# Splitting expert weights one job per main step, with four result buffers

## The chip, the cores and the metric

The kernel runs on one core of one Trainium2 chip. The metric is device time in microseconds (us) of one execution; for the kernel before it is the median of 3 runs. The core's engines are named as the profile names them: PE (matmul) and PEld (its weight loads), DVE (VectorE), ACT (ScalarE), POOL (GpSimd) and SP (SyncE), which here issues nearly all DMA transfers.

## The reference, cut to what matters

Three layers follow each other. The first is a spectral filter along the sequence, the second a mixture of 8 experts with one expert per token, the third a dense MLP.

```python
X = np.fft.rfft(x, axis=1)                       # x: 8 x 3072 x 256
Yr = Xr @ w_r - Xi @ w_i + b_r
Yi = Xr @ w_i + Xi @ w_r + b_i
# soft threshold of both at 0.01, then irfft -> 24576 tokens of 256
expert_idx = np.argmax(xn @ en.T / tau, axis=1)
out[mask] = gate_w[mask, None] * (relu(x[mask] @ w1[e]) @ w2[e])   # w1: 8x256x1024, w2: 8x1024x256
g = leaky_relu(x @ w_in)                          # w_in: 256x2048
return g @ w_out
```

## The kernel before, in words

Products are made nearly exact in fp32 by splitting each operand into a rounded high part and a remainder (three matmuls for each product). The experts' weights are split once, by the kernel itself, in the shadow of the spectral layer: 128 jobs, 16 for each expert, each of one 128x256 block.

The spectral layer goes over 8 batches. A batch b has a **main stage** of 26 steps g (`main_step`, three of which, g = 0, 1, 2, are merged into the end of the stage before) and a **transform stage** of 37 steps n2. Every engine works its instructions off in the order in which they are written, SP's queue too: a transfer that has to wait holds all that is written behind it.

A main step g writes, in this order: `mix(g)`, six matmuls `pu` (L490), whose result ACT copies to `uh` (L178) and DVE subtracts to `ul` (L179); `s2(g-1)`, six matmuls `py` (L512) from `uh` and `ul`, then on DVE `z` (L515), `t` (L516) and `z` again (L517); from g = 24 on two `s1` of the next batch (matmuls `ps`, L468, which read that batch's input `xt`); `s2i(g-2)`, matmuls `pz` (L528) from `z`, with an ACT copy to `Z` (L531) in every second step; two small operations of the list `todo` (the gates of the batch before: a square root at L687 in step 3 and an exponential at L691 in step 5, both on ACT, and some DVE work); one `scatter`, or two where g is a multiple of 3 (POOL: a 1x1 copy `dummy` at L655 that waits for the step's `z`, then an indirect DMA `xs` at L656, which writes rows of the batch before to their slots in DRAM); then the **split jobs**; and in steps 21 to 24 of batches 1 to 6 `refill(b + 1, 0..3)`, which has SP load the first four pieces of the next batch's input (`load_x`, L369). Four more pieces are loaded in the transform stage. A batch's last two scatters are in its successor's transform stage.

A call of `split_job` has SP load a block `wf` (L451, 128 KB, three buffers). The call also works on the block that was loaded two calls earlier: ACT copies it to the high half of `hl` (L456), POOL subtracts for the low half (L457), and SP stores `hl` to DRAM (L458, 256 KB). So the load of a block waits for the subtraction of the block three jobs earlier, and the ACT copy into a buffer of `hl` for the store that last read this buffer: with two buffers, the store of two jobs earlier.

In batch 0 there is one call in each of the steps 4 to 25. From batch 1 on the calls are in steps 3 to 13: two in odd steps and one in even ones, 17 in a batch. Batch 0 does 22 jobs, batches 1 to 6 do 102, batch 7 the last 4. After the spectral layer come 103 expert blocks and 48 MLP tiles, which the change doesn't touch.

Of the kernel before, what the change touches and what calls it, by code (L numbers as in the profile page):

```python
# [12 lines left out]
F32R = mybir.dt.float32r  # L13
# [130 lines left out]
def build(ctx: ExitStack, tc: tile.TileContext, a: dict, out: bass.AP):  # L144
# [183 lines left out]
    def spectral(big, expert_start):  # L328
        with ExitStack() as st, ExitStack() as mst:
# [4 lines left out]
            m2 = mst.enter_context(tc.tile_pool(name="m2", bufs=2, side="right"))  # L334
# [62 lines left out]
            def prologue3():  # L397

                emb = rp.tile([E, D], F32, tag="lg", name="emb")
                trif = rp.tile([N1, 224], F32, tag="inc", name="trif")  # L400
                esq = rp.tile([E, D], F32, tag="ex", name="esq")
                en2 = rp.tile([E, 1], F32, tag="en2", name="en2")
                dma = lambda o, i: lambda: nc.sync.dma_start(o, i)

                def norm():
                    nc.scalar.activation(esq, emb, AF.Square, accum_out=en2)
                    nc.scalar.activation(en2, en2, AF.Sqrt)
                    nc.vector.tensor_scalar(en2, en2, 1e-6, None, op0=ALU.add)
                    nc.vector.reciprocal(en2, en2)
                    nc.vector.tensor_scalar(emb, emb, en2, None, op0=ALU.mult)  # L410

                def trans():

                    nc.vector.tensor_copy(identr, ident)
                    nc.vector.memset(en, 0.0)
                    pe_ = psb.tile([128, 2, E], F32, tag="b", name="pe_")
                    for db in range(2):
                        nc.tensor.transpose(pe_[:, db, :], emb[:, 128 * db:128 * db + 128], ident[:E, :E])
                    nc.vector.tensor_copy(en[:, :, 0:E], pe_)

                def init():
                    nc.vector.tensor_copy(tri, trif)
                    nc.vector.reciprocal(tau, tau)
                    nc.vector.memset(carry, 0.0)
                    nc.vector.memset(used, 0.0)

                return ([dma(emb, a["moe_expert_emb"]), dma(ident, a["ident"]),
                         dma(tau, a["moe_tau"][None, :].to_broadcast([128, 1])), norm,
                         dma(trif, a["tri"]), dma(scan, a["scan"]), dma(eord, a["eord"]), dma(li, a["li"]),
                         trans, init])  # L430
# [16 lines left out]
            def split_job():  # L447
                if jobs:
                    src, dst, o = jobs.pop()
                    wf = m3.tile([128, 256], F32, tag="wf", name="wf")  # L450
                    nc.sync.dma_start(wf, src)  # L451
                    wait.append((wf, dst, o))
                if len(wait) == 3 or not jobs and wait:
                    wf, dst, o = wait.pop(0)
                    hl = m2.tile([128, 2, 256], F32R, tag="hl", name="hl")
                    nc.scalar.activation(hl[:, 0], wf, AF.Copy)  # L456
                    nc.gpsimd.tensor_tensor(hl[:, 1], wf, hl[:, 0], op=ALU.subtract)  # L457
                    nc.sync.dma_start(dst.rearrange("p (s n) -> p s n", s=2)[:, :, o:o + 256], hl.bitcast(F32))  # L458
# [3 lines left out]
            def s1(b, n2, later=None):  # L462
                q, r = divmod(n2, 4)
                if n2 % 2 == 0:
                    ps1[0] = psa.tile([128, 2, 2, 96], F32, tag="a", name="ps1")
                p = ps1[0]
                for cb in range(2):
                    nc.tensor.matmul(p[:, n2 % 2, cb, :], xt[b, q][:, r, 128 * cb:128 * cb + 128],  # L468
                                     f1, start=True, stop=True)
                if n2 % 2 == 1:  # L470
                    src = p.rearrange("p n c j -> p c j n")
                    h = AH[:, :, :, n2 - 1:n2 + 1]
                    nc.scalar.activation(h, src, AF.Copy)
                    low = lambda: nc.vector.tensor_tensor(AL[:, :, :, n2 - 1:n2 + 1], src, h, op=ALU.subtract)
                    if later is None:
                        low()
                    else:
                        later.append(low)
# [3 lines left out]
            def mix(g):  # L482
                p = psa.tile([128, 512], F32, tag="a", name="pu")
                ops = []
                for cb in range(2):
                    ah = AH[:, cb, 4 * g:4 * g + 4, :].rearrange("p j n -> p (j n)")
                    al = AL[:, cb, 4 * g:4 * g + 4, :].rearrange("p j n -> p (j n)")
                    ops += [(ah, wh[:, cb]), (ah, wl[:, cb]), (al, wh[:, cb])]
                for i, (l, r) in enumerate(ops):
                    nc.tensor.matmul(p, l, r, start=(i == 0), stop=(i == 5))  # L490
                uh = m2.tile([128, 512], F32R, tag="uh", name="uh")
                ul = m2.tile([128, 512], F32R, tag="ul", name="ul")
                split_evict(uh, ul, p)
                U[g] = (uh, ul)
# [3 lines left out]
            def s2(g):  # L498
                uh, ul = U.pop(g)
                p = psb.tile([128, D], F32, tag="b", name="py2")  # L500
                if g == 0:
                    o1, o2 = 0, 128
                else:
                    o2 = 256 + (g - 1) * 192
                    o1 = o2 + 64
                ops = []
                for o, c in ((o1, 0), (o2, 256)):
                    ops += [(g2h[:, o:o + 128], uh[:, c:c + 256]),
                            (g2h[:, o:o + 128], ul[:, c:c + 256]),
                            (g2l[:, o:o + 128], uh[:, c:c + 256])]  # L510
                for i, (l, r) in enumerate(ops):
                    nc.tensor.matmul(p, l, r, start=(i == 0), stop=(i == 5))  # L512
                z = m2.tile([128, D], F32, tag="z", name="z", bufs=3)
                t = mp.tile([128, D], F32, tag="t", name="t")
                nc.vector.tensor_tensor(z, p, bt0 if g == 0 else bt, op=ALU.add)  # L515
                nc.vector.tensor_scalar(t, z, LAM, -LAM, op0=ALU.min, op1=ALU.max)  # L516
                nc.vector.tensor_tensor(z, z, t, op=ALU.subtract)  # L517
                Y[g] = z
# [3 lines left out]
            def s2i(g):  # L522
                y = Y.pop(g)
                if g % 2 == 0:
                    pz[0] = psc.tile([128, 2, 2, 128], F32, tag="c", name="pz")
                p = pz[0]
                for db in range(2):
                    nc.tensor.matmul(p[:, db, g % 2, :], y[:, 128 * db:128 * db + 128], gi[:, g, :],  # L528
                                     start=True, stop=True)
                if g % 2 == 1:  # L530
                    nc.scalar.activation(  # L531
                        Z[:, :, :, 4 * g - 4:4 * g + 4],
                        p.rearrange("p b g (j n) -> p b n (g j)", n=N2), AF.Copy)
# [294 lines left out]
            def main_step(b, g):  # L828
                last = b == B - 1
                if g == 3:  # L830

                    s2i(0)
                if g < NG:
                    mix(g)
                if 1 <= g <= NG:
                    s2(g - 1)
                if g >= NG and not last:
                    for _ in range(2):
                        s1(b + 1, lead[0])
                        lead[0] += 1  # L840
                if g >= 3:
                    s2i(g - 2)
                if b == 0 and g == 3:
                    todo.extend(prologue3())
                if g >= 3:
                    for _ in range(2):
                        if todo:
                            todo.pop(0)()
                if 2 <= g <= NG:
                    for _ in range(1 if g % 3 else 2):  # L850
                        scatter(Y[g - 1][0:1, 0:1])
                if g >= 4 if b == 0 else 3 <= g < 14:
                    split_job()
                    if b and g % 2:
                        split_job()
                if b == 0 and g % 3 == 1 and g // 3 < 8:
                    load_x(1, g // 3)
                if b and g in (21, 22, 23, 24):
                    refill(b + 1, g - 21)
# [340 lines left out]
```

## Time and profile before

| | |
|---|---|
| median of 3 runs | 4411.87 us (4411.73 to 4413.19) |
| profiled execution | 4420.32 us |
| its span in the trace | 4418.6 us |
| PE busy | 4293.5 us, 97% |
| DVE, ACT, POOL busy | 53%, 43%, 13% |
| spectral layer | about the first 1000 us of the span |

The table is read with the stages in mind: 97% for PE is a mean in which the long expert and MLP stages outweigh the spectral layer, where the change is.

### The profile page before, as it was taken

The numbers are of one execution on the slowest core, as the hardware profiler recorded it, in microseconds if no ns is written. First come the engines' busy times: TensorE is split into PE (matmuls) and PEld (weight loads), VectorE is DVE, ScalarE is ACT, GpSimd is POOL, SyncE is SP. The second block draws the span as 40 slices with busy tenths as digits, with TensorE's granted clock in tenths as the row PEclk, the third lists the DMA queues.
The fourth block names the chain that finished last, engine by engine and source line by source line (L and its number), as shares of the span: only waits on it lengthen the run. The fifth ranks groups of instructions, "written<-read, shape, count | busy, mean of one in ns | idle before, by whom it ended". The sixth has DMA issues, their size and how long they took to land.

```text
span 4418.6 us, 72633 instructions
## 1 busy us (share of the span) xinstructions
PE 4293.5 (97%) x27214; PEld 3813.2 (86%) x27214; DVE 2363.5 (53%) x4977; ACT 1891.4 (43%) x4268; POOL 595.1 (13%) x893
## 2 busy tenths in 40 slices
PE   9888889899999999999999999999999999999999
PEld 8777777779999999999978888888888888888888
DVE  5666666664455555543345555555555555555554
ACT  4455555443333333333344444444444444444443
POOL 2333333432100000000020001010100101010000
PEclk9999999999999999999999999999999999999999
DMA  7333333342332233433210000000000000000000
GB/s 217 100 113 94 93 99 99 117 144 95 107 109 86 94 137 131 170 120 117 85 40 20 29 20 25 24 25 24 23 27 20 26 23 25 24 24 25 20 20 15
DMA packets 139075, 309.72 MB, mean 70 GB/s; under 512 B 21049, under 2 KB 72866, under 8 KB 134370
## 3 DMA queue, kind: packets, MB, share of 16 engines
q1 hardware_dynamic: 113250, 244.34, 16.4%
q0 software_dynamic: 25472, 60.73, 4.6%
q8 instruction: 215, 3.52, 0.3%
q14 instruction: 138, 1.13, 0.1%
HBM read 542.30 MB, written 115.02 MB: 149 GB/s over the span
## 4 chain that ended last, share of the span: by engine, by line
PE 86%; DVE 4%; DMA 3%; issue 3%; ACT 2%; POOL 1%; another core or an unknown queue 0%; SPq 0%; ACTq 0%; POOLq 0%; DVEq 0%
PE mpH L1037 24%; PE mpO L1062 16%; PE pO L272 13%; PE pH L256 13%; PE mpO L1063 8%; PE pu L490 3%; PE py L512 1%; PE ps L468 1%; PE pz L528 1%; DMA w2d<-hl 1%; PE pyo L576 1%; DMA w1d<-hl 1%; DVE vl L543 1%; ACT uh L178 1%; PE pT L240 1%
## 5 line engine op out<-in xcount | busy, mean ns | idle before, releaser
L1062 PE MATMUL mpO<-W,mgh 128*128 128x512 f32 x3008 | 1096.5, 399 | 0.0
L1043 DVE TENSOR_TENSOR mg<-mpH,ms 128x512 f32<-128x512 f32 x768 | 531.2, 692 | 1047.8 <-ACT ms L1042 1043.1
L1037 PE MATMUL mpH<-mxh,W 128*128 128x512 f32 x3072 | 1083.5, 394 | 5.9 <-DVE mg L1043 4.7
L1042 ACT ACTIVATE ms<-mpH 128x512 f32<-128x512 f32 x768 | 459.9, 599 | 1191.0 <-PE mpH L1037 972.7
L1063 PE MATMUL mpO<-W,mgl 128*128 128x256 f32 x3008 | 842.3, 280 | 0.0
L256 PE MATMUL pH<-xh,W 128*128 128x256 f32 x3296 | 729.9, 284 | 3.2 <-issue 1.9
L1037 PEld LDWEIGHTS mpH<-mxh,W 128*128 128x128 f32 x3072 | 578.7, 188 | 146.0 <-DVE mg L1043 5.4
L1062 PEld LDWEIGHTS mpO<-W,mgh 128*128 128x128 f32 x3008 | 564.7, 188 | 132.5
L260 DVE SCALAR_TENSOR_TENSOR ehl<-pH,ehh 128x256 fp32r<-128x256 f32 x824 | 349.4, 424 | 606.4 <-ACT ehh L259 592.4
L259 ACT ACTIVATE ehh<-pH 128x256 fp32r<-128x256 f32 x824 | 316.4, 384 | 766.6 <-PE pH L256 754.6
L272 PE MATMUL pO<-W,ehh 128*128 128x256 f32 x3264 | 630.5, 285 | 0.0
L1037 PE MATMUL mpH<-mxl,W 128*128 128x512 f32 x1536 | 606.4, 395 | 0.0
L1063 PEld LDWEIGHTS mpO<-W,mgl 128*128 128x128 f32 x3008 | 567.3, 189 | 24.5
L256 PEld LDWEIGHTS pH<-xh,W 128*128 128x128 f32 x3296 | 574.2, 192 | 4.2 <-issue 1.8
L1010 POOL DMA_INDIRECT mxr<-ys,row x192 | 186.6, 972 | 2871.2 <-PE mpT L1022 1748.1
L1052 DVE TENSOR_TENSOR mgl<-mg,mgh 128x512 fp32r<-128x512 f32 x768 | 523.1, 681 | 0.0
L272 PEld LDWEIGHTS pO<-W,ehh 128*128 128x128 f32 x3264 | 508.7, 192 | 0.0
L1051 ACT ACTIVATE mgh<-mg 128x512 fp32r<-128x512 f32 x768 | 479.4, 624 | 0.1
L256 PE MATMUL pH<-xl,W 128*128 128x256 f32 x1648 | 467.1, 283 | 0.4 <-issue 0.4
L272 PE MATMUL pO<-W,ehl 128*128 128x256 f32 x1632 | 462.3, 283 | 0.0
L256 PEld LDWEIGHTS pH<-xl,W 128*128 128x128 f32 x1648 | 316.9, 192 | 1.2 <-issue 1.2
L1037 PEld LDWEIGHTS mpH<-mxl,W 128*128 128x128 f32 x1536 | 289.7, 189 | 32.7 <-issue 0.4
(214 smaller groups left out, 5370.2 us busy)
## 6 DMA issues: line engine op xcount, KB each, us to landing
W<-w1d SPq DMA_DIRECT2D x101, 2048.0 KB
W<-w2d SPq DMA_DIRECT2D x101, 2048.0 KB
xg<-xs SPq DMA_DIRECT2D x103, 256.0 KB
ys<-eo SPq DMA_DIRECT2D x102, 256.0 KB
xt<-in_x_dram SPq DMA_DIRECT2D x64, 384.0 KB
out_dram<-mo SPq DMA_DIRECT2D x47, 512.0 KB
wf<-in_moe_w_dram SPq DMA_DIRECT2D x128, 128.0 KB
w1d<-hl SPq DMA_DIRECT2D x64, 256.0 KB
```

What stands on the lines that cost most here:

```text
L256: nc.tensor.matmul(p, l, r, start=(i == 0), stop=(i == 5))
L259: nc.scalar.activation(hh, p, AF.Relu)
L260: nc.vector.scalar_tensor_tensor(hl, p, 0.0, hh, op0=ALU.max, op1=ALU.subtract)
L272: nc.tensor.matmul(O[b][:, t, :], l, r, start=(f == 0 and i == 0 and t == 0), stop=(f == 7 and i == 2 and t == 1))
L1010: nc.gpsimd.indirect_dma_start(out=xr[i][:, t].bitcast(F32), out_offset=None, in_=ys, in_offset=IndirectOffsetOnAxis(ap=slot[:, 4 * i + t: ...
L1037: nc.tensor.matmul(p, l, r, start=(j == 0), stop=(j == 5))
L1042: nc.scalar.activation(s, p, AF.Copy, scale=0.01)
L1043: nc.vector.tensor_tensor(g, p, s, op=ALU.max)
L1051: nc.scalar.activation(gh, g, AF.Copy)
L1052: nc.vector.tensor_tensor(gl, g, gh, op=ALU.subtract)
L1062: nc.tensor.matmul(p, gh[:, c], wout[:, :, f], start=(f == 0), stop=False)
L1063: nc.tensor.matmul(p[:, 0], gl[:, c], wout[:, 0, f], start=False, stop=(f == 15))
```

## The change

The single calls stay in steps 4 to 22 of batch 0 (23 to 25 go), and from batch 1 on there is one call in each of the steps 3 to 22, in place of 17 calls in steps 3 to 13. Batch 0 then does 19 jobs, batches 1 to 5 do 100, and batch 6 the last 9, with two more calls that only finish loaded blocks. `hl` gets four buffers, so that an ACT copy waits for the store of four jobs earlier.

```diff
-                    hl = m2.tile([128, 2, 256], F32R, tag="hl", name="hl")
+                    hl = m2.tile([128, 2, 256], F32R, tag="hl", name="hl", bufs=4)
...
-                if g >= 4 if b == 0 else 3 <= g < 14:
+                if 4 - (b > 0) <= g < 23:
                     split_job()
-                    if b and g % 2:
-                        split_job()
                 if b == 0 and g % 3 == 1 and g // 3 < 8:
                     load_x(1, g // 3)
                 if b and g in (21, 22, 23, 24):
                     refill(b + 1, g - 21)
```

## Rows read from the trace of the kernel before

**Rows 1.** The page, part 2: PE's busy tenths in 40 equal slices.
```profile
PE   9888889899999999999999999999999999999999
```
**Rows 2.** Windows from a batch's uh(3) to uh(23), L178 alone: stretch, length, busy.
```profile
core 0: us, ACT busy (x), PEclk, DMA share, GB/s
143.25:216.63 73.38, 11.66 (x20) 0.95 0.48 145
...
767.28:838.12 70.84, 11.63 (x21) 0.95 0.50 151
sum 429.60, ACT 69.80; mean ACT 11.63
...
55.97:89.16 33.19, 7.78 (x14) 1.00 0.67 202
894.50:952.38 57.88, 11.87 (x21) 1.00 0.35 114
```
**Rows 3.** Tile hl, whole span: durations, then what ended waits (us, times).
```profile
L456 ACT ACTIVATE hl<-wf x128: 399/417/424, 48.4 to 911.4; 128x256 fp32r<-128x256 f32 x128
...
  DMA w1d<-hl: 92.7, 37
  DMA w2d<-hl: 91.7, 38
```
**Rows 4.** Chain of waits, batch 2, main and transform stage: start, us, what.
```profile
283.21 2.38 DMA w2d<-hl
...
356.62 4.08 DMA xt<-in_x_dram
```
**Rows 5.** Timeline of ACT, steps 3 to 5 of batch 2 (idle before in brackets).
```profile
269.13 0.57 ACT L178 ACTIVATE uh<-pu 128x512 fp32r<-128x512 f32 x1
...
270.52 1.28 ACT L687 ACT_TABLE_LOAD   x1
...
271.95 0.71 ACT L456 ACTIVATE hl<-wf 128x256 fp32r<-128x256 f32 x2
272.56 0.57 ACT L178 ACTIVATE uh<-pu 128x512 fp32r<-128x512 f32 x1
277.92 0.42 ACT L456 ACTIVATE hl<-wf 128x256 fp32r<-128x256 f32 x1 [4.78 <-DMA w1d<-hl]
...
279.32 1.28 ACT L691 ACT_TABLE_LOAD   x1
```
**Rows 6.** Timeline of POOL, DVE and PE, steps 21 to 24 of batch 2.
```profile
336.76 0.17 POOL L655 COPY dummy<-z 1x1 f32<-1x1 f32 x1 [0.93 <-DVE z L517]
...
337.46 0.93 POOL L656 DMA_INDIRECT xs<-xt,si  x1 [0.53 <-issue]
...
338.73 0.92 POOL L656 DMA_INDIRECT xs<-xt,si  x1 [0.16 <-issue]
...
340.98 0.29 DVE L516 TENSOR_SCALAR t<-z 128x256 f32<-128x256 f32 x1
...
341.37 1.03 PE L468 MATMUL ps<-f,xt 96*128 96x96 f32 x8
```
**Rows 7.** Timelines of PE, POOL and DVE, steps 4 to 8 of batch 2.
```profile
276.74 1.10 PE L528 MATMUL pz<-gi,z 128*128 128x128 f32 x4 [1.96 <-DVE z L517]
...
287.57 0.74 POOL L457 TENSOR_TENSOR hl<-wf,hl 128x256 fp32r<-128x256 f32 x1
...
287.71 0.76 DVE L516 TENSOR_SCALAR t<-z 128x256 f32<-128x256 f32 x1
...
289.06 0.17 POOL L655 COPY dummy<-z 1x1 f32<-1x1 f32 x1 [0.75 <-DVE z L517]
```
**Rows 8.** Timeline of SP's queue, end of batch 2's split jobs.
```profile
317.06 0.54 SPq L458 DMA_DIRECT2D w1d<-hl  x1
317.65 0.60 SPq L451 DMA_DIRECT2D wf<-in_moe_w_dram  x1
...
322.58 1.80 SPq L369 DMA_DIRECT2D xt<-in_x_dram  x4
```

## The prediction, made before the change was run

> **What bounds the kernel now.** I read the page first. PE is busy nine tenths or more in most slices, but only eight tenths in slices 2 to 6 and in slice 8 [rows 1]; a slice is 110 us, so the holes lie in the spectral layer, where the change is. PE ends nearly everything else, and what the split jobs do can only be paid for, or won, in those holes.
>
> Next I took the pace of the main stage from the starts of `uh`, one in each step. In batch 0, with one job in each step and no scatters, 13 steps take 33.19 us, 2.55 each [rows 2]. That is the free pace: PE's own work. From batch 1 on the 20 steps from uh(3) to uh(23) would take 51.0 us at it. Batches 1 to 6 take 429.60 us together (the first and the last of six stretches stand in the rows), 123.6 more than 6 x 51.0. Batch 7, with only four jobs and the two finishing calls, takes 57.88, an excess of 6.9. So **130.5 us** of stalls lie in the steps that hold split jobs or follow them.
>
> The waits of tile `hl` name the cause: before its ACT copy, ACT sat idle for 92.7 + 91.7 us until a store of `hl` had landed, in 75 of 128 copies [rows 3]. The chain of waits shows one link: a store, 2.38 us from issue to landing, that releases the copy [rows 4]. With two buffers and three jobs in two steps, a copy waits for a store that POOL's subtraction made possible only just before. Behind the copy on ACT stands the next `uh`, behind that `ul`, `py` and PE.
>
> **What goes.** With four buffers a copy waits for the store of four jobs earlier, four steps or 10.2 us at the free pace. From `uh` to the end of a subtraction it takes, at two scatters, 6.2 us (below), and the store 2.4 more: 8.6, under 10.2. The whole wait of [rows 3] goes, in batches 1 to 7. I don't book its 184 us, since much of it overlaps work, but the 130.5 us of lost pace, and then subtract what stays or comes new.
>
> **What stays: the gates.** In step 3 ACT loads a table for the square root, 1.28 us, and makes two hl copies in 0.71; uh(4) comes 3.43 after uh(3), 0.9 late. In step 5 the exponential brings another table load of 1.28 [rows 5]. Neither goes with the change; only one copy of the two does. `z` is late behind `ul` too: PE waited 1.96 us for it in step 5 [rows 7]. Bounds for a batch: 0.9, the lateness of the one step, and 6.9, batch 7's whole excess with six jobs over two buffers. From 6.9 the wait for a store goes, 4.78 in the like place [rows 5], which leaves 2.1; I take 3.2 for what POOL still does to `z` there. Seven batches: 22.4.
>
> **What is new: POOL and SP in every step.** In three steps (7.65 us) POOL has four scatters and three subtractions. A scatter right behind another takes 1.27 (337.46 to 338.73), one after a wait 0.17 + 0.53 + 0.93 = 1.63 [rows 6]; a subtraction takes 0.74 [rows 7]. Run back to back that is 4 x 1.27 + 3 x 0.74 = 7.3, which just fits. With a wait ahead of each step's first scatter it is 8.4, and every step 0.25 longer: 17 steps, 4.2 a batch. POOL that lags runs back to back, so it should settle near the first. A `wf` load stands behind the store (0.59 apart on SP [rows 8]) and so behind a subtraction: 6.2 + 0.6 after `uh`, and with the 2.4 of the larger `hl` store as an upper bound it lands at 9.2. ACT needs it three steps on, and can start that copy as late as 2.1 behind its `uh` (2.55 less 0.42 for the copy [rows 3]), 9.75, so it fits by 0.5.
>
> There is a coupling to DVE: `t` takes 0.29 when free [rows 6], and 0.76 when it starts with a subtraction of 0.74 running; it ends 0.16 behind it [rows 7]. At the free pace `t` begins 1.7 after `uh`. The subtractions then lie 0.4, 2.4 or 1.9 into a step, so that only the third, in the step after next, comes near it, from behind. The Trainium skill (SBUF — State Buffer, "Who interferes with whom") says that a GpSimd instruction and a tensor_scalar in a two-port mode take the shared port pair whole, and that whoever comes second waits until the first is done. The trace agrees (0.76 against 0.29). By that rule a step in which the subtraction comes first loses up to 0.74 on DVE; where all do, it is the last rival below.
>
> For all of this I take 1.5 a batch, between 0 (batch 0 hides a job in every step) and 5 (4.2 plus a collision here and there). Five batches: 7.5. Batch 6 has jobs only to step 13; its share lies within the 3.2.
>
> **What is moved: the first input loads.** In steps 21 and 22 a call now stands ahead of the `refill` on SP, and its store waits for that step's subtraction. Before, SP had nothing left behind step 13's calls; four loads were issued at 322.58 [rows 8], 18.8 us ahead of the first `s1` at 341.37 [rows 6]. After, in batch 2's times with steps 21 to 23 already free: the second scatter of step 21 ends at 338.73 + 0.92 = 339.65, the subtraction 0.74 later at 340.4, 6.2 after uh(21) at 334.19 (uh(23) less two steps). The store goes out, and the first load 0.59 behind it, at 341.0. A first load of 384 KB took 4.08 from issue to landing [rows 4], which gives 345.1. PE wants it at 341.37 and is 3.7 us late; behind it wait all `ps` and the whole transform stage, which has nothing to catch up with. After idle time PE also starts slowly: the granted clock is 0.95 in the stretches with stalls against 1.00 without [rows 2]; I add an estimate of 0.5. So 4.2 in batches 1 to 5; batch 6 has done its jobs by then. Bounds 1.5 (the load lands in 2.4, as the smaller store does, and half of the rest is absorbed) and 5.5 (POOL lags by a further scatter). Five batches: 21. The later load of step 22 lands behind a stage that is shifted as far, and costs nothing more.
>
> **Nothing:** three calls fewer in batch 0, where PE waited little; two small `todo` operations in each of batch 6's steps, which DVE has room for; the four buffers themselves; the expert and MLP stages, which get the same data and start later or earlier as a whole.
>
> **The sum.** 130.5 - 22.4 - 7.5 - 21 = 79.6. The profiled execution took 4420.3 us, its span 4418.6; less 79.6 that is 4340.7. The median lies 8.4 below the profiled execution, so the forecast is 4411.9 - 79.6 = **4332** us, 1.8% faster.
>
> **The rivals.**
> - *The input load is hidden.* If SP or the load is quicker than I work out, or the transform stage has slack, the 21 us stay won: 4311. For it: the four loads were issued in a burst when they took 4.08, and a lone one may be quicker. Against: SP's order, and the need at 341.37.
> - *POOL becomes the bound.* If every step's first scatter pays the 0.53 of restart, or `wf` lands late, steps take 2.8 or a little more: 17 steps of 0.25 to 0.4 over five batches, 21 to 34 instead of 7.5: 4346 to 4359. For it: 7.3 of 7.65. Against: the restart cost vanishes when POOL lags.
> - *The loop through the shared port* (the other side). If each subtraction blocks the next step's `t`, the loop is: subtraction ends, rest of `t` and `z` 0.75 until `dummy` starts [rows 7], `dummy` to the end of the scatter 1.63, subtraction 0.74: 3.12, and 4.39 with two scatters. Twenty steps, seven of them double, take 71.3 instead of 51.0. Batches 1 to 5 then lose 20.3 + 4.2 each, where they lose 20.8 on average now (the 123.6 less batch 6's 19.8, over five): 18.5 us worse. Batch 6 with 11 such steps (39.4 against 28.1, a loss of 11.3) gains 8.5, batch 7 3.7. The gates' 3.2 comes on top in batches 1 to 6, 19: in all 4437. It decides at about three in four of the steps: the 130.5 less 21 (loads) and 22.4 (gates) over 111 steps is 0.78 a step, and a locked step costs 1.02. For it: `t` at 0.76 beside a subtraction. Against: once PE is slower, `t` is ready while POOL still scatters, and slips in ahead.
>
> **How the numbers follow.** Chances: forecast 0.48 (its own range 4318 to 4345), hidden load 0.27, POOL as the bound 0.20, the loop 0.05. The likeliest gives 4332. The range goes from the hidden load with gates and lag at the kind end (4311 less 9) to POOL as the bound with some collisions (4362), 4302 to 4362, leaving some 2 in 10 out on both sides. A change under 0.2% (9 us) could not be told from none; only the loop reaches there, whole or in part, so faster 0.95, same 0.02, slower 0.03.
>
> **What the changed profile would show.** Copies of `hl` no longer released by stores. `uh` every 2.55 us from about step 7 to step 23, and 54 to 57 us from uh(3) to uh(23) in batches 1 to 6. In batches 1 to 5, and not in 6, PE idle for 3 to 4 us ahead of the first `ps`, released by `xt`. `t` mostly at 0.29. The forecast is wrong if steps 8 to 22 run at 2.8 or more, if `t` is often near 1 us, if copies wait for `wf`, or if the wait ahead of `ps` is absent or above 5 us.

## The result, and the profile after

The changed kernel takes 4367.36 us (median of 4 runs, 4364.93 to 4374.58) against 4412.53 us for the kernel before, measured again on the same chip: ratio 0.9898, 95% interval 0.9881 to 0.9916. It is 45 us faster, where 80 were forecast (4332, range 4302 to 4362), and lies outside the range by 5 us. The main stages came out within 4 us of the forecast; the stretch behind them cost two and a half times what I had put down for it.

The same slices of the page as [rows 1], for the changed kernel: the holes in the spectral layer are fewer, not gone.

```profile
PE   9989898999999999999999999999999999999999
```

The windows of [rows 2] in the changed kernel, L178 alone, from uh(3) to uh(23) of batches 1 to 6 (first, last and sum), then of batch 7. Columns: stretch, its length, busy time (count), granted clock, DMA share, GB/s.

```profile
141.82:196.48 54.66, 11.80 (x21) 1.00 0.56 173
...
745.10:799.48 54.38, 11.86 (x20) 1.00 0.49 148
sum 338.82, ACT 70.84; mean ACT 11.81
...
851.84:903.03 51.19, 11.91 (x20) 1.00 0.28 90
```

The sum fell from 429.60 to 338.82, batch 7 from 57.88 to 51.19: 97.5 us are won here. 33.0 us of excess over the free pace are left (338.82 - 306, and 0.2 in batch 7); the forecast had 29.9.

Tile `hl` after, what ended its waits (us, times), against [rows 3]: no store is in the list any more. In its place stand the loads of `wf`.

```profile
  DMA wf<-in_moe_w_dram: 63.8, 56
  ACT hl L456: 31.3, 15
  issue: 6.8, 6
```

What was won is half given back behind uh(23). These are windows of PE from uh(23) of a batch to uh(3) of the next, first the kernel before, batches 1 to 6 (first, last, sum):

```profile
216.63:269.13 52.50, 49.13 (x402) 1.00 0.17 47
...
838.12:894.50 56.38, 53.39 (x402) 0.91 0.17 44
sum 321.65, PE 300.56; mean PE 50.09
```

and then the changed kernel, all six:

```profile
196.48:262.62 66.14, 57.23 (x402) 0.85 0.26 74
318.64:384.16 65.52, 57.75 (x402) 0.84 0.26 74
441.04:500.91 59.87, 51.89 (x402) 0.94 0.29 81
561.10:626.29 65.19, 57.94 (x402) 0.84 0.27 74
682.98:745.10 62.12, 53.15 (x402) 0.92 0.27 78
799.48:851.84 52.36, 49.16 (x402) 1.00 0.17 45
sum 371.20, PE 327.12; mean PE 54.52
```

Batches 1 to 5 lose 53.6 us together (318.8 against 265.3); batch 6, which has no split job after step 13, loses nothing, and even lacks the low clock that the kernel before shows there (4.0). The place is seen in the timelines of batch 2, of POOL, SP and PE in turn, which answer to [rows 6] and [rows 8]:

```profile
319.62 0.74 POOL L457 TENSOR_TENSOR hl<-wf,hl 128x256 fp32r<-128x256 f32 x1
...
320.38 0.54 SPq L458 DMA_DIRECT2D w1d<-hl  x1
321.22 0.35 SPq L369 DMA_DIRECT2D xt<-in_x_dram  x1
...
325.80 2.02 PE L468 MATMUL ps<-f,xt 96*128 96x96 f32 x8 [4.92 <-DMA xt<-in_x_dram]
```

The order is the one forecast: subtraction, store, first input load, and PE waiting for it. The wait is 4.94, 4.92, 4.47, 3.97 and 5.39 us in batches 1 to 5, 23.7 together. What was forecast far too small is seen in the row's duration: eight matmuls take 2.02 us, where the same eight took 1.03 in [rows 6]. Windows of PE in batch 2 (the fourth number is the granted clock) show why:

```profile
320.60:325.80 5.20, 0.28 (x3) 0.76 0.77 227
325.80:340.00 14.20, 14.20 (x69) 0.50 0.33 103
340.00:351.30 11.30, 10.22 (x93) 0.99 0.32 89
```

Behind the wait PE runs at 0.50 of its clock, 1.2 GHz, for 14 us, busy throughout. Over the five stretches PE idles 22.8 us more than before and is busy 30.9 us more, with the same work. The books of the profiled executions: 130.5 of stalls before, less 33.0 left, less 53.6 behind uh(23), plus 4.0 in batch 6, is 47.9; the spans differ by 51.9, the other 4 being small shifts ahead of batch 1 and after the spectral layer. The medians differ by 45.2.

### The profile page after: what moved, and what is told of

It reads as the page before. It is cut to its first block, busy times and chain, and to the rows that moved or that the text cites. A ratio compares the mean times of both kernels' runs of the same rounds, so it can differ in the third digit from the quotient of the medians.

```text
span 4366.7 us, 72634 instructions
## 1 busy us (share of the span) xinstructions
PE 4271.0 (98%) x27214; PEld 3819.4 (87%) x27214; DVE 2391.4 (55%) x4977; ACT 1895.8 (43%) x4268; POOL 601.2 (14%) x893
## 4 chain that ended last, share of the span: by engine, by line
PE 88%; DVE 5%; DMA 2%; issue 2%; ACT 1%; POOL 1%; SPq 0%; another core or an unknown queue 0%; DVEq 0%; POOLq 0%; ACTq 0%
PE mpH L1035 24%; PE mpO L1060 16%; PE pO L272 14%; PE pH L256 14%; PE mpO L1061 8%; PE pu L490 3%; PE ps L468 2%; PE py L512 1%; PE pz L528 1%; DMA xt<-in_x_dram 1%; PE pyo L576 1%; DVE t L516 1%; DVE z L517 1%; DVE vl L543 1%; PE pT L240 1%
```

## The experiments

Theory A: the first input load is late because it stands on SP behind the split stores of steps 21 and 22, and PE's idling brings the low clock on top. Rivals: the transfers themselves are slow there (B); the clock falls for another reason than the wait (C). For the main stages, theory W says that the waits for `wf` make up what is left there, and rival P that POOL does. The ratios are to the kernel before on the same chip, which took 4399.5 to 4411.4 us in these series. "Main" is the sum from uh(3) to uh(23) over batches 1 to 6 (306 at the free pace), "behind" the sum from uh(23) to the next uh(3); both are of one execution each, the profiled one.

| kernel | ratio (95% interval) | main, us | behind, us |
|---|---|---|---|
| before | 1 | 429.6 | 321.6 |
| changed | 0.9898 (0.9881 to 0.9916) | 338.8 | 371.2 |
| e1 loads early | 0.9822 (0.9804 to 0.9841) | 351.8 | 329.4 |
| e2 pace only | 0.9961 (0.9947 to 0.9976) | 365.2 | 360.7 |
| e3 buffers only | 0.9894 (0.9878 to 0.9911) | 384.1 | 320.2 |
| e4 kept warm | 0.9864 (0.9847 to 0.9880) | 338.4 | 357.7 |
| e5 one step ahead | 0.9799 (0.9783 to 0.9816) | 334.8 | 331.2 |
| e6 calls to 18 | 0.9786 (0.9770 to 0.9803) | 337.3 | 318.7 |
| e7 four blocks | 0.9873 (0.9856 to 0.9890) | 335.6 | 367.2 |
| e8 both | 0.9766 (0.9749 to 0.9782) | 329.6 | 319.1 |
| e9 idle long | 0.9908 (0.9892 to 0.9925) | 335.7 | 368.5 |
| e10 idle short | 0.9864 (0.9847 to 0.9881) | 335.8 | 354.8 |

**Loads early.** From the changed kernel:

```diff
+                if b and g in (17, 18, 19, 20):
+                    refill(b + 1, g - 17)
                 if 4 - (b > 0) <= g < 23:
                     split_job()
...
-                if b and g in (21, 22, 23, 24):
-                    refill(b + 1, g - 21)
```

> The changed kernel with the four refill loads of a batch written in steps 17 to 20, ahead of each step's split job, in place of steps 21 to 24 behind it. Theory A (the order on SP delays the first input load, PE idles ahead of the first ps for 4.0 to 5.4 us in batches 1 to 5, and then runs at a granted clock of 0.50 for some 14 us): the wait ahead of ps goes, the stretch from uh(23) to the next uh(3) falls from 60 to 66 us to the 52.5 of batch 6, and about 54 us go: 4313 (4305 to 4325). Rival B (the loads are late because subtractions, wf loads and stores now run up to the end of the stage and the transfers themselves are slow): a wait of 3 us or more stays and the time is above 4345. Rival C (the clock falls because the whole stage has less idle and more load, not through the wait): the wait goes, the granted clock of the transform stage stays below 0.9, and the time is about 4343.

The wait ahead of the first `ps` is gone and "behind" falls by 42 us, against rival B. But the input loads now stand among the `wf` loads on SP, and the main stages grow by 13 us. ACT's timeline in steps 18 to 21 of batch 2:

```profile
299.98 0.42 ACT L456 ACTIVATE hl<-wf 128x256 fp32r<-128x256 f32 x1 [2.38 <-DMA wf<-in_moe_w_dram]
...
307.92 0.42 ACT L456 ACTIVATE hl<-wf 128x256 fp32r<-128x256 f32 x1 [2.38 <-DMA wf<-in_moe_w_dram]
```

So the gain over the changed kernel is 0.8% where 1.2% was expected, and the time, 4336 us, lies above the expected range. In three of the later stages the clock falls here too, as it does now and then in the kernel before.

**The two edits apart.** "Pace only" gives `hl` two buffers again; "buffers only" is the kernel before with four.

```diff
-                    hl = m2.tile([128, 2, 256], F32R, tag="hl", name="hl", bufs=4)
+                    hl = m2.tile([128, 2, 256], F32R, tag="hl", name="hl")
```

> The changed kernel with two buffers for hl again: one call in each step, nothing else. If the wait for the store is what sets the pace (from uh to the end of a subtraction 6.2 us, the store 2.4 more, over two steps), steps run at about 4 us instead of 2.8, 20 steps lose about 29 us a batch where before 17 calls in 11 steps lost 20.8, and the late input load stays: 4440 (4410 to 4480), slower than before. If the spreading alone gives the gain and the buffers are spare, 4367 as the changed kernel.

```diff
-                    hl = m2.tile([128, 2, 256], F32R, tag="hl", name="hl")
+                    hl = m2.tile([128, 2, 256], F32R, tag="hl", name="hl", bufs=4)
```

> The kernel before with four buffers for hl and its old calls, 17 in steps 3 to 13. If the waits for the stores were all of the cost, the main stages get as short as in the changed kernel (54 to 57 us from uh(3) to uh(23)) and no input load is late: 4315. If POOL and the three wf buffers take the place of the store when three jobs come in two steps, steps 3 to 13 run at 3.5 to 4 us, copies wait for wf loads, and the time is about 4385 (4360 to 4405). In both cases no wait ahead of the first ps.

With the pace alone, copies still wait for stores, as tile `hl` shows, but the main stages lose 59 us where 174 (29 a batch) had been expected: steps follow each other at about 4.5, 2.0 and 2.7 us, three in 9.2, not at 4 each. The time is 4394 us where 4440 was expected, 0.4% faster than the kernel before and not slower. I had let every copy wait for the store of the slowest step.

```profile
  DMA w1d<-hl: 70.5, 43
  DMA w2d<-hl: 67.0, 41
```

With the buffers alone there is no wait ahead of `ps` and no wait for a store; ACT now waits for `wf` and for POOL:

```profile
  DMA wf<-in_moe_w_dram: 69.1, 53
  ACT hl L456: 36.6, 22
  POOL hl L457: 16.6, 15
```

The main stages win 45.5 us, nearly the whole gain: the kernel is as fast as both edits together, whose larger gain in the main stages is paid back behind them. The measured time lies below the 4385 of the expectation and within its bounds.

**Kept warm.** To part the clock from the wait, PE gets something to do while it waits:

```diff
+                if g == NG and 1 <= b <= 5:
+                    pk = psc.tile([128, 512], F32, tag="c", name="pk")
+                    for _ in range(18):
+                        nc.tensor.matmul(pk, wh[:, 0, :128], wh[:, 0], start=True, stop=True)
                 if g >= NG and not last:
```

> The changed kernel with 18 extra matmuls of 512 columns in step 24 of batches 1 to 5, ahead of the first s1; their result is not used. They fill some 4.1 us of the 4.0 to 5.4 us in which PE waits for the input. Theory A (the low clock behind the wait is the price of PE's idling): the wait in sum stays (PE busy in its place), but the granted clock behind it stays at 1.00, ps takes 0.58 instead of 1.01, and about 24 us go: 4343 (4335 to 4352). If the clock falls for another reason, or the idle time is the whole loss, no gain: 4367 or, where the extra matmuls are late themselves, up to 4375.

Windows of PE, 14.2 us from the first `ps` of batches 1 to 5:

```profile
204.47:218.67 14.20, 13.93 (x125) 1.00 0.35 104
317.75:331.95 14.20, 13.52 (x124) 1.00 0.42 117
435.73:449.93 14.20, 13.93 (x131) 1.00 0.27 80
553.49:567.69 14.20, 14.20 (x100) 0.76 0.34 105
675.32:689.52 14.20, 14.01 (x125) 1.00 0.39 112
```

The input is as late as before, yet the clock stays at 1.00 in four of five batches (in the changed kernel such windows show 0.51, 0.50, 0.82, 0.58 and 0.71). 13.5 us of "behind" go, where about 24 were expected, and the time, 4352 us, lies at the edge of the expected range. In batch 4 a wait of 1.4 us is left ahead of the first `ps`, and the clock falls behind it; in batches 4 and 5 it falls later in the stage, behind waits of 1.8 and 3.3 us for the second set of input loads.

**Idling alone.** Two kernels on top of "calls to 18" (below), where no input is late: POOL makes six (in the short one `range(3)`, three) extra subtractions on a scratch block, and PE reads the last one ahead of `ps`; nothing else uses it.

```diff
+                if g == NG and 1 <= b <= 5:
+                    pk = psc.tile([128, 512], F32, tag="c", name="pk")
+                    nc.tensor.matmul(pk, hold[0][:, :128], wh[:, 0], start=True, stop=True)
...
+                if g == NG - 1 and 1 <= b <= 5:
+                    hold[0] = mp.tile([128, 256], F32R, tag="hold", name="hold")
+                    for _ in range(6):
+                        nc.gpsimd.tensor_tensor(hold[0], wh[:, 0, :256], wl[:, 0, :256], op=ALU.subtract)
```

> The kernel with calls to step 18 (no late input load), in which PE is made to wait for nothing useful: in step 23 of batches 1 to 5 POOL makes six extra subtractions on a scratch block, ahead of its scatter, and in step 24 one extra matmul, not used, reads their result ahead of the first ps. The input is long there. If PE's idling itself costs the clock, PE idles about 4 us ahead of ps and then runs at a granted clock of 0.50 for some 14 us: the stretch from uh(23) to the next uh(3) goes from 52.5 to about 61 us in five batches, 45 us over the kernel with calls to step 18, about as slow as the changed kernel (ratio to the kernel before 0.989). If the clock falls only where DMA traffic or subtractions run beside PE at that time, only the idle time shows: 20 us over it, ratio 0.983.

> The same with three extra subtractions, so that PE idles about 1.8 us. If the price of the clock comes with any wait, 9 us of idling and about 25 of the clock in five batches, ratio 0.986. If it comes only with longer waits, as the waits of 1 to 2 us for the later input load let one think, the clock falls in one or two of the five batches and the ratio is 0.981 to 0.983.

The long one, PE's timeline in batch 2, the matmul that waits:

```profile
322.21 0.80 PE L839 MATMUL pk<-wh,hold 128*128 128x512 f32 x1 [4.36 <-POOL hold L855]
```

and the window of PE behind it:

```profile
322.21:336.41 14.20, 14.20 (x72) 0.54 0.07 21
```

With hardly any DMA traffic beside it (share 0.07), the clock falls in all five batches. They lose 49.7 us behind uh(23) against "calls to 18", 22.6 of it waiting (4.77 + 4.36 + 4.35 + 4.77 + 4.35) and 27.1 besides, 5.4 a batch: some 3 us of that are the extra matmuls themselves, the rest is the same work at the low clock. This is the changed kernel's loss, made by hand with no late input and hardly any DMA traffic, and together with "kept warm" it rules out rival C. The short one waits 1.9 us in each batch; of the windows behind, three show a clock near 0.52 and two 1.00, of which one each:

```profile
320.12:334.32 14.20, 14.20 (x70) 0.52 0.07 21
437.04:451.24 14.20, 13.93 (x125) 1.00 0.10 29
```

It costs almost what the reading "with any wait" had forecast (0.986), though the clock does not fall every time: in the two batches that kept it, a later wait for input of 3.1 and 1.4 us is followed by a dip of the clock.

**One step ahead.** Only the order of two statements in the changed kernel is exchanged:

```diff
+                if b and g in (21, 22, 23, 24):
+                    refill(b + 1, g - 21)
                 if 4 - (b > 0) <= g < 23:
                     split_job()
...
-                if b and g in (21, 22, 23, 24):
-                    refill(b + 1, g - 21)
```

> The changed kernel with refill written ahead of split_job in the same steps 21 to 24, so that the first input load stands behind the store of step 20's call and no longer behind that of step 21's. Theory A (the place on SP sets the delay, step by step): the load goes out about one step, 2.6 us, earlier; the wait ahead of the first ps falls from 4.0 to 5.4 to about 2.1 us in batches 1 to 5, 13 us in all, and what the clock takes behind it (now about 25 us) stays or goes with it: 4340 (4328 to 4355). Rival B (the transfers are slow in that stretch wherever the load stands): the wait stays above 3.5 us, 4365.

One place earlier on SP does more than the expectation: the wait ahead of the first `ps` is 0.51 us in batch 1, none in batch 2, and 0.53, 0.80 and 0.21 in batches 3 to 5. The second piece still comes late, by 0.37 to 2.20 us. The longest of these waits, in batch 2, brings the low clock back; the rows are the first `ps` of batch 1, the second piece's in batch 2, and the window of PE behind that:

```profile
200.03 1.13 PE L468 MATMUL ps<-f,xt 96*128 96x96 f32 x8 [0.51 <-DMA xt<-in_x_dram]
...
314.37 1.17 PE L468 MATMUL ps<-f,xt 96*128 96x96 f32 x4 [2.20 <-DMA xt<-in_x_dram]
...
314.37:322.90 8.53, 8.53 (x43) 0.50 0.35 115
```

Batch 2 takes 60.8 us from uh(23) to the next uh(3), the other four 53.5 to 54.2. "Behind" is 40 us shorter than in the changed kernel, and the time, 4314 us, lies below the expected range. The transfers are no quicker: the second load of batch 1 takes 4.46 us from issue to landing, where the first of batch 2 in the changed kernel took 4.54. So rival B is out: the place on SP decides.

**Calls to 18, four blocks, both.** Each from the changed kernel, the third with both edits:

```diff
-                if 4 - (b > 0) <= g < 23:
+                if 4 - (b > 0) <= g < (19 if b else 23):
```

> The changed kernel with the calls of batches 1 to 7 in steps 3 to 18 in place of 3 to 22; refill stays in steps 21 to 24. Batch 7 then does 13 jobs. Theory A: the last store leaves SP before step 21, no wait ahead of the first ps, the stretch from uh(23) to the next uh(3) is 52.5 but for dips of the clock that the kernel before has too; the main stages of batches 1 to 6 keep their 2 to 6 us of excess, batch 7 gets 4: 4318 (4308 to 4332). If the loads are late for another reason, above 4345.

```diff
-                    wf = m3.tile([128, 256], F32, tag="wf", name="wf")
+                    wf = m3.tile([128, 256], F32, tag="wf", name="wf", bufs=4)
...
-                if len(wait) == 3 or not jobs and wait:
+                if len(wait) == 4 or not jobs and wait:
```

> The changed kernel with four buffers for wf, and each block worked on three calls after its load. Theory W (what is left over the free pace in steps 7 to 23, 4.7 us a batch, is the copy's wait for its wf load, 63.8 us in 56 copies): these waits go, the main stages of batches 1 to 5 fall from 55 to 60 to about 53 us, some 20 us go, the late input load stays: 4347 (4338 to 4357). Rival P (POOL sets the pace of these steps, the wait for wf only moves with it): the steps stay at 2.7 to 2.8 on average, 4365.

> Calls in steps 3 to 18 from batch 1 on, and four buffers for wf with each block worked on three calls after its load. Theories A and W together: no late input load, and main stages of about 53 us in batches 1 to 6: 4300 (4290 to 4315), faster than both kernels. Under rival P as the kernel with calls to step 18 alone, 4318.

With calls to step 18, "behind" is 318.7, a little under the kernel before, and the ratio 0.9786 is what 4318 would be to 4412.5. Four blocks take the `wf` waits of tile `hl` from 63.8 us to next to nothing,

```profile
  ACT hl L456: 34.2, 16
  DMA wf<-in_moe_w_dram: 3.3, 5
```

but the main stages only from 338.8 to 335.6. The time, 4348 us, is the one that theory W gave, but not for its reason: the main stages of batches 1 to 6 take 55.2 to 56.5 us each where W wanted 53, and against the kernel before, which took 4400.6 in this series, the gain over the changed kernel is only 0.25%. Theory W falls. In place of the waits a plain beat appears, two steps of 2.55 us and one of 3.2 to 3.3. DVE and POOL at one long step of that kernel:

```profile
295.94 0.92 POOL L656 DMA_INDIRECT xs<-xt,si  x1 [0.16 <-issue]
...
296.37 1.41 DVE L516 TENSOR_SCALAR t<-z 128x256 f32<-128x256 f32 x1
...
296.87 0.74 POOL L457 TENSOR_TENSOR hl<-wf,hl 128x256 fp32r<-128x256 f32 x1
```

`t`, 0.29 us when free, begins 0.5 ahead of POOL's subtraction, while a scatter is under way, and ends 0.17 behind the subtraction; `z` comes late for `pz`, and the step is 0.7 longer. From uh(7) to uh(23) in batches 1 to 6 of this kernel, 22 of the `t` overlap a subtraction that began behind them and take 0.8 to 1.5 us; 20 of the 32 steps of 3 us or more follow one of these. Beside a scatter alone `t` takes 0.29 to 0.48. So rival P is right about where the cost lies, in the form of a meeting of POOL and DVE once in three steps. That the meeting makes the step long is read from the rows; no run took it away. Both edits together are the fastest kernel of the study, 0.9766, 2.3% under the kernel before and 1.3% under the changed one. Their main stages, 329.6, lie between what W (six times 53, 318) and P (as with calls to step 18, 337) gave: there four blocks are worth 7.7 us, 5.8 of them in batches 3 and 4. The time, 4301 us, is the one that A and W together gave, but again against 4400.6 for the kernel before.

## Why the prediction was wrong

- **The bound** was read rightly: the waits for stores went to zero, and the 130.5 us of lost pace could be won. The two edits share it: buffers alone win 45.5 us in the main stages, the pace alone 64.4, both 90.8.
- **The gates** were put at 22.4 us in seven batches and cost 7.5, taken from uh(3) to uh(7) against four free steps: about 1.5 us in each of batches 2 to 6, where the two table loads take 2.56, and nothing in batches 1 and 7.
- **POOL and SP in every step** were put at 7.5 and cost 25.5 (uh(7) to uh(23)). Two things were read wrongly. The `wf` loads, which were to fit by 0.5, are waited for in 56 copies; in "four blocks", without these waits, the stretch still costs 22. And I had let the third subtraction come near `t` from behind, at no cost. It does come from behind, but `t` then ends behind it, and the step is up to 0.7 longer. By the rule of the Trainium skill cited in the prediction (SBUF — State Buffer, "Who interferes with whom") whoever comes second waits until the first is done; that does not settle this row, in which `t` began behind the scatter but ahead of the subtraction. What holds `t` there is not shown. This error and that of the gates cancel to 3 us, by luck.
- **The moved input loads** are the term that failed: 21 us, measured 53.6, or 10.7 a batch against bounds of 1.5 and 5.5. The mechanism was right in place, order and batches. The wait is 4.7 us on average where I had 3.7: POOL lagged by 0.9 in step 21 (the subtraction begins 6.4 and not 5.5 after `uh`), and the load took 4.54 instead of 4.08. The larger error is one sentence: "After idle time PE also starts slowly ... I add an estimate of 0.5". Idling cost, beside the wait itself, not 0.5 but 6.0 a batch here (29.9 us in five) and some 5 in the kernel that only idles. The windows with a clock of 0.95 against 1.00 had shown the effect; I averaged it over a stage and did not look up what one wait in that stage cost.
- **The rivals:** the hidden load and the loop through the shared port did not happen; POOL as the bound did in part, with a long step once in three.
- **Nothing** for batch 0, the buffers and the later stages holds within the 4 us of the books.

The trace of the kernel before had rows that warn of this price. In batch 2 PE waits 1.63 us for a later input load, the clock falls behind it, and the stretch from uh(23) to the next uh(3) takes 54.56 us where batch 1's takes 52.50. That is 2.1 us, of which the longer wait explains 0.6. The waits of 1.02, 1.37, 1.49 and 0.85 us in batches 1, 3, 4 and 5 are followed by no fall, that of 1.43 in batch 6 is:

```profile
360.84 0.66 PE L468 MATMUL ps<-f,xt 96*128 96x96 f32 x4 [1.63 <-DMA xt<-in_x_dram]
...
361.00:367.00 6.00, 6.00 (x41) 0.72 0.40 107
```

## What to carry to other kernels

When calls are spread over more of a stage, list what stands behind them on each in-order queue at the new end of the stage: here the first of four input loads, issued 19 us ahead of its use before, came 4 to 5.4 us late. Price a new wait of PE with the clock behind it, read from a row behind a wait of like length, and not by the idle time alone. And before adding buffers against a wait, see what the wait hides: the `wf` waits were 64 us in the list, and taking them away won 3 us of the main stages (8 with calls to 18).

## What was not expected of the hardware

The clock's price. A wait of 4.4 to 4.8 us of PE, made with extra subtractions on POOL and one extra matmul, was followed by 14 us at a granted clock of 0.53 to 0.61 in all five batches; a wait of 1.9 us by a clock of 0.52 or 0.53 in three batches of five and of 1.00 in two. Eighteen matmuls whose result nobody reads, put in the place of the idle time, kept it at 1.00 in four of five. And `t` beside POOL: it began 0.5 us ahead of the subtraction, during the scatter, and still ended only behind it.
